# Attention, experts and a gated unit in one kernel: more weight blocks decoded beside the experts, splits and decoding put ahead of each chunk's results, six plain units for nine

## The chip, the cores and the metric

The kernel runs on one core of one Trainium2 chip. The metric is the device time of one execution in microseconds. Five engines work side by side, each through its own list of instructions in order: TensorE (PE: matmuls, with PEld for its weight loads), VectorE (DVE), ScalarE (ACT), GpSimd (POOL) and SyncE (SP), which here issues most of the DMA transfers. An engine that reaches an instruction whose data are not there waits, and so does everything behind it in its list.

## The reference

Causal attention with a decay bias over 4 x 8 heads of 576 positions, a layer that sends each of the 2304 rows to one of 8 experts, and a gated unit. Only the last two are touched:

```python
def _moe_ref(x, w_gate, w1, w2):            # x: 2304 x 512
    ...
    for e in range(E):                      # 8 experts
        xe = x[expert_idx == e]
        h = np.maximum(xe @ w1[e], 0.0)     # 512 x 1024
        ye = h @ w2[e]                      # 1024 x 512
        out[mask] = gate_w[mask, None] * ye

def _moe2_ref(x, w_gate, w_val, w_out, rms_g):
    xn = x / rms * rms_g
    g = xn @ w_gate                         # 512 x 1536
    silu = g * (1.0 / (1.0 + np.exp(-g)))
    val = xn @ w_val
    return (silu * val @ w_out).astype(np.float32)
```

`w_gate`, `w_val` and `w_out` of the gated unit arrive as 64-bit floats.

## The kernel before

**Stages.** Attention, then `moe` (expert 0, then `for s in range(1, E)`), then `glu` (the products with `w_gate` and `w_val` and the gating) and `glu_rest` (the product with `w_out`). On ACT, DVE and PE, and on SP for most of the program, the instructions stand in the order in which the Python code issues them. In `glu` each step is put into a plan with a due time by `add(at, ...)`, and the plan is issued in order of due time; POOL follows it there too.

**Every fp32 product is three passes** (`PASSES`): each operand is split into a rounded high part (a cast on ACT) and a rest (a subtraction on DVE or POOL, always called the rest here).

**Experts.** Expert s multiplies its `CAP[s-1]` rows (312, 304, 300, 292, 284, 268, 248) by w1 in eight `gemm1` groups f = 0..7 and by w2 in four `gemm2` chunks c = 0..3. In between the weights of expert s+1 come in eight pieces of 512 KB: `feed` issues a load into one of four staging buffers (`STG = 4`, used in turn), `split` casts a piece on ACT and calls `rest` for the piece before it on DVE. The rows of expert s+1 are transposed on PE after chunks 1 and 2 (`x_transpose`: high part on ACT, rest on DVE); `gemm1` of expert s+1 begins right after chunk 3 and needs all four column groups of them.

**64-bit blocks.** A block of 128 x 512 64-bit weights is loaded whole (512 KB) and made to 32-bit floats by `decoding`: four DVE operations (steps 0, 1, 3, 4) and an absolute value on ACT (step 2). Beside the experts `decode_words` takes blocks from the same staging buffers and sends the 32-bit result to DRAM (`keep_words`, 256 KB); five are done so before the change, one per expert 1 to 5. The remaining ones are decoded where they are used. The gated unit needs twelve pairs of blocks f = 0..11 (`w_gate` and `w_val`).

**Gated unit.** Rows are three groups p = 0..2 of 768. A unit (p, f) makes 128 columns of gate and value for one group. A plain unit does eight products of six matmuls (`WHOLE`); the other form does seven (`SEVEN`), with sums of x blocks (S1 to S4, `x_sums`, split by `x_rests`) and of weight blocks (`w_sum`), and adds up results on DVE (`glu_step`: u2, u3, c22, c21, c12). `PLAIN` lists the plain units; `UNITS` is the order. The list `START` gives the due times: 8 for a plain unit, 7 for the other. S1 lies in the buffer of A21, which plain units still read, and the sums of group 2 are made from a second load into the buffer of group 0 (`ringa`).

Of the kernel before, what the change touches and what calls it, by code (L numbers as in the profile page):

```python
# [7 lines left out]
F32 = mybir.dt.float32  # L8
# [11 lines left out]
E = 8  # L20
# [15 lines left out]
NF = F2 // 128  # L36
# [747 lines left out]
def keep_words(k, m, f, t):  # L784
    out = k.wo32[f // 2 - 2][:, f % 2, :] if m == 2 else k.wg32[:, m, :]
# [223 lines left out]
def moe(k, close):  # L1009
# [6 lines left out]
    k.order = [(s, u, q) for s in range(1, E) for u in range(4) for q in (0, 2)]  # L1016
# [53 lines left out]
    for s in range(1, E):  # L1070
# [50 lines left out]
WORDS_AT = 6 + 6  # L1121
# [6 lines left out]
A21 = S1  # L1128
PLAIN = ((0, 0), (0, 1), (1, 0), (1, 1), (2, 0), (2, 1), (0, 2), (1, 2), (2, 2))
UNITS = (list(PLAIN) + [(p, f) for f in range(3, NF - 2) for p in range(3)]  # L1130
# [124 lines left out]

def w_decode(k, f, n):
# [5 lines left out]
def w_parts(k, f):  # L1262
    if f == 0:
        return k.flat[:, 0, :], None, k.flat[:, 1, :], None
# [3 lines left out]
def w_sum(k, f, n):  # L1268
    g, gl, v, vl = w_parts(k, f)
# [90 lines left out]
def glu_head(k):  # L1360
    def dec(f, m, *parts):
        for n in parts:
            decoding(k, k.raw[f, m])[n]()

    V, G = k.nc.vector, k.nc.gpsimd
    k.raw, k.ps = {}, {}
    k.flat = staging(k, [2, 512], F32)
    k.nc.sync.dma_start(out=k.flat, in_=k.wg32)
    yield
    w_load(k, 1, 0)  # L1370
    yield
    w_load(k, 1, 1)
    yield
# [3 lines left out]
    yield  # L1377
    w_cast(k, 0, 0)
    yield
    dec(1, 0, 0, 1)  # L1380
    yield
    w_rest(k, 0, 0, G)
    dec(1, 0, 2)
    yield
    for n in (1, 4):
        w_cast(k, 0, n)
    yield
    dec(1, 0, 3, 4)
    for n in (1, 4):
        w_rest(k, 0, n, G)  # L1390
    yield
    yield
    yield
    x_cast(k, 0, "A11")
    x_rest(k, 0, "A11", V)
    dec(1, 1, 0, 1)
# [659 lines left out]
```

## Time and profile before

| | us |
|---|---|
| median of three timed runs | 848.31 (846.22 to 851.0) |
| profiled execution: its own time | 841.21 |
| its span | 839.5 |
| mean granted TensorE clock in it | 0.994 of full speed |

The span runs from the first to the last profiled instruction; 1.7 us of the execution lie around it. In the rows below, "idle before <-X" is the time an engine stood still before an instruction and what released it. PE's matmuls overlap at their ends, so the distance from one start to the next tells more than a duration.

### The profile page before, as it was taken

Reading aid. Unit: us, or ns where it says so; the run is one execution under the profiler, and the core shown is the slowest. Engines: PE = TensorE matmul, PEld = TensorE weight load, DVE = VectorE, ACT = ScalarE, POOL = GpSimd, SP = SyncE. Lnnn points to the kernel's source line nnn. Section 1 sums busy time; section 2 is a strip of 40 time slices with the busy share of each in tenths; the row PEclk is TensorE's granted clock in tenths of the full one; section 3 lists DMA queues with packets and bytes.
Section 4 is the critical chain, followed back from the end, with each engine's and each line's share of the span. In section 5 each row is a group of like instructions: output and inputs, shape, how many; then the busy total and the mean of one; then the engine's idle time right before and its main releaser. Section 6 shows DMA issues by size and latency. Waiting matters only on the chain.

```text
span 839.5 us, 15787 instructions
## 1 busy us (share of the span) xinstructions
PE 818.7 (98%) x5622; PEld 748.2 (89%) x5622; DVE 640.0 (76%) x1425; ACT 462.7 (55%) x1060; POOL 226.5 (27%) x249
## 2 busy tenths in 40 slices
PE   7999999999999999999999999999999999999994
PEld 4777767789899999999999999999999998899994
DVE  6557688965767767867698988888898969868880
ACT  5988988875756566566453443333333335453440
POOL 3335845342000000000131232544343352032120
PEclk9999999999999999999999999999999999999997
DMA  7999978246567576767651433323233375344510
GB/s 226 301 317 304 320 245 270 101 133 203 182 200 247 182 226 198 230 224 219 239 197 48 148 104 107 111 104 107 88 107 107 108 280 173 99 151 145 158 52 30
DMA packets 79757, 146.72 MB, mean 175 GB/s; under 512 B 7424, under 2 KB 44315, under 8 KB 79667
## 3 DMA queue, kind: packets, MB, share of 16 engines
q1 hardware_dynamic: 76707, 136.08, 51.1%
q0 software_dynamic: 2912, 9.46, 3.0%
q8 instruction: 46, 0.75, 0.4%
q14 instruction: 44, 0.36, 0.1%
q10 hardware_dynamic: 48, 0.07, 0.0%
HBM read 108.04 MB, written 37.54 MB: 173 GB/s over the span
## 4 chain that ended last, share of the span: by engine, by line
PE 92%; DVE 3%; ACT 1%; DMA 1%; issue 1%; SPq 0%; POOL 0%; POOLq 0%; ACTq 0%; DVEq 0%
PE gg L1314 29%; PE g L935 12%; PE g L912 12%; PE gp L1772 10%; PE go L1707 6%; PE t L370 5%; PE s L307 5%; PE pvy L416 5%; PE tl L444 2%; PE sm L338 2%; PE xp L883 1%; DMA ringa<-ytd 1%; PE r L984 1%; PE r L973 1%; ACT pt L403 0%
## 5 line engine op out<-in xcount | busy, mean ns | idle before, releaser
L935 PE MATMUL g<-h,u 128*128 128x256 f32 (+7 forms) x768 | 105.0, 295 | 0.0
L912 PE MATMUL g<-xt,u 128*128 128x256 f32 (+7 forms) x768 | 104.2, 295 | 0.0
L912 PEld LDWEIGHTS g<-xt,u 128*128 128x128 f32 x768 | 101.4, 189 | 0.8
L935 PEld LDWEIGHTS g<-h,u 128*128 128x128 f32 x768 | 101.2, 189 | 0.5
L1291 POOL TENSOR_TENSOR ws<-raw,ws 128x512 fp32r<-128x512 f32 (+1 forms) x25 | 33.0, 1335 | 220.4 <-ACT ws L1286 220.4
L744 ACT CAST u<-raw 128x1024 fp32r<-128x1024 f32 x62 | 65.1, 1050 | 19.5 <-DMA raw<-in_w 19.5
L351 ACT ACTIVATE p<-sc,nm 128x128 f32<-128x128 f32 (+3 forms) x128 | 71.3, 582 | 6.8 <-DVE nm L295 6.8
L757 DVE TENSOR_TENSOR u<-raw,u 128x1024 fp32r<-128x1024 f32 x58 | 70.5, 1218 | 0.4 <-ACT u L744 0.4
L1314 PE MATMUL gg<-gx2a,ws 128*128 128x384 f32 x360 | 67.4, 336 | 0.6 <-DVE tmp L1336 0.6
L1314 PE MATMUL gg<-gx0a,ws 128*128 128x384 f32 x360 | 67.7, 336 | 0.0
L1314 PE MATMUL gg<-gx1a,ws 128*128 128x384 f32 x360 | 67.1, 335 | 0.0
L1314 PEld LDWEIGHTS gg<-gx2a,ws 128*128 128x128 f32 x360 | 62.8, 188 | 0.9 <-DVE tmp L1336 0.9
L1314 PEld LDWEIGHTS gg<-gx0a,ws 128*128 128x128 f32 x360 | 63.1, 188 | 0.0
L1314 PEld LDWEIGHTS gg<-gx1a,ws 128*128 128x128 f32 x360 | 62.7, 188 | 0.0
L1352 POOL TENSOR_TENSOR hs<-tmp,hs 128x384 f32<-128x384 f32 x27 | 30.2, 1120 | 106.3 <-ACT hs L1350 106.3
L403 ACT COPY pt<-t 128x512 f32<-128x512 f32 (+3 forms) x160 | 56.1, 454 | 3.1 <-PE t L370 2.0
L370 PE MATMUL t<-ident,p 128*128 128x128 f32 x400 | 52.2, 275 | 0.0
L370 PEld LDWEIGHTS t<-ident,p 128*128 128x128 f32 x400 | 44.5, 140 | 8.4 <-DVE nm L295 8.3
L1693 POOL DMA_INDIRECT out<-raw,oid x18 | 20.5, 1139 | 111.9 <-DVE raw L1794 64.5
L416 PE MATMUL pvy<-pt,vp 128*64 128x512 f32 (+4 forms) x320 | 47.5, 428 | 0.7 <-ACT pt L403 0.7
L1332 ACT COPY tmp<-gg 128x384 f32<-128x384 f32 x27 | 13.0, 481 | 57.2 <-PE gg L1314 55.5
L1242 ACT ACTIVATE raw<-raw 128x512 f32<-128x512 f32 x31 | 21.2, 682 | 36.0 <-DVE raw L1240 35.9
(391 smaller groups left out, 1812.3 us busy)
## 6 DMA issues: line engine op xcount, KB each, us to landing
raw<-in_w SPq DMA_DIRECT2D x64, 512.0 KB
hd<-hs SPq DMA_DIRECT2D x72, 192.0 KB
xs<-zrow SPq DMA_DIRECT2D x8, 771.0 KB
raw<-in_wo SPq DMA_DIRECT2D x12, 512.0 KB
raw<-in_wg SPq DMA_DIRECT2D x12, 512.0 KB
raw<-in_wv SPq DMA_DIRECT2D x12, 512.0 KB
vp<-in_v SPq DMA_DIRECT2D x16, 320.0 KB
in<-cumd SPq DMA_DIRECT2D x20, 256.0 KB
```

The lines of the kernel that those rows point to most:

```text
L307: k.nc.tensor.matmul(ps[h], st.q[r, 128 * i:128 * i + 128], st.k[r, 0:w], start=True, stop=p >= BYPE)
L351: k.nc.scalar.activation(out, st.s[i, h][:, 0:w], AF.Exp, bias=st.nm[:, n:n + 1], scale=-1.0, accum_out=acc)
L370: nc.tensor.transpose(ps[:, off:off + 128], src[:, 128 * j:128 * j + 128], k.ident)
L403: nc.scalar.copy(b, a)
L416: nc.tensor.matmul(st.y[r, a - 64:512], st.v[:, h, j, :], k.pt[:, h, o:o + S - a], start=j == 0, stop=j == 4)
L744: nc.scalar.copy(w[:, :, 0, :], raw)
L757: k.nc.vector.tensor_tensor(w[:, :, 1, :], raw, w[:, :, 0, :].bitcast(F32), op=ALU.subtract)
L912: nc.tensor.matmul(ps[:, 0:n], w[:, f % 4, a, 128 * kc:128 * kc + 128], x[b][:, kc, 0:n], start=kc == 0 and i == 0, stop=kc == 3 and i == 2)
L935: nc.tensor.matmul(ps[:, 0:n], w[:, f % 4, a, 128 * c:128 * c + 128], k.h[b][:, f, 0:n], start=f == 0 and i == 0, stop=f == 7 and i == 2)
L1314: k.nc.tensor.matmul(k.ps[u, bank], w[:, a, 128 * c:128 * c + 128], x[:, b, GT * c:GT * c + GT], start=first and c == 0 and n == 0, stop=c ...
L1707: k.nc.tensor.matmul(k.acc[tau], c[:, a, 128 * t:128 * t + 128], w[:, b, :], start=f == 0 and i == 0, stop=f == NF - 1 and i == 2)
L1772: k.nc.tensor.matmul(k.acc[i, bank], t[:, a, j, :], item_weight(k, j, w, b), start=first and j == 0 and n == 0, stop=j == 5 and n == 2, sk ...
```

## The change

It has three parts.

**More blocks beside the experts.** Eleven blocks instead of five are decoded in `moe`: the three of `w_out` and both blocks of f = 0..3 (`WORDS = 4`). Experts 1 to 5 take two each, at c = 0 and c = 2, expert 6 takes one. The order of pieces (p) and blocks (w) is the string `PIECES_AND_WORDS`. In `glu`, f = 0..3 are then loaded as 32-bit floats (`words_load`).

**Order within an expert.** The split of a chunk, and steps 0 and 1 of a block, are now issued ahead of `gemm2` of the same chunk, so on ACT and DVE they stand ahead of that chunk's results; step 2 stands behind them, and steps 3 and 4 with the store at the next odd chunk.

**Six plain units.** (0, 2), (1, 2) and (2, 2) move from the plain form to the other one. The sums of x blocks, the weight sums of f = 2 and the second load for group 2 move some 20 due-time units ahead.

```diff
 def decode_words(k):
     s, m, f, raw = k.staged.pop(0)
-    for step in decoding(k, raw)[0:3]:
+    steps = decoding(k, raw)
+    for step in steps[0:2]:
         step()
+    yield
+    steps[2]()
     yield
     rest(k)
     compact(k, raw, raw)
...
-    words = [(E, 2, f) for f in range(4 + EARLY_OUT, NF)] + [(E, 0, 0), (E, 1, 0)]
-    for n, item in enumerate(words):
-        k.order.insert(WORDS_AT + 9 * n, item)
-    chain = iter(())
+    pieces = [(s, u, q) for s in range(1, E) for u in range(4) for q in (0, 2)]
+    words = [(E, 2, f) for f in range(4 + EARLY_OUT, NF)] + [(E, m, f) for f in range(WORDS) for m in range(2)]
+    k.order, chain = [(words if c == "w" else pieces).pop(0) for c in PIECES_AND_WORDS], iter(())
...
         for c in range(4):
+            if c % 2:
+                next(chain, None)
+            split(k, 1, c % 2 == 0)
+            if c % 2 == 0 and k.staged and k.staged[0][0] == E:
+                chain = decode_words(k)
+                next(chain)
             gemm2(k, s, c, n)
-            next(chain, None)
-            if c == 1:
-                split(k)
+            if c % 2 == 0:
+                next(chain, None)
...
-            split(k)
-            if c == 0 and s <= len(words):
-                chain = decode_words(k)
-                next(chain)
+            if c % 2:
+                feed(k)
+            if c == 1:
+                split(k)
...
-WORDS_AT = 6 + 6
+WORDS = 4
+PIECES_AND_WORDS = "pppppp" + "pp" + 5 * ("ppp" + "pwpppwp") + "ppp" + "pwpppp"
...
-PLAIN = ((0, 0), (0, 1), (1, 0), (1, 1), (2, 0), (2, 1), (0, 2), (1, 2), (2, 2))
+PLAIN = ((0, 0), (0, 1), (1, 0), (1, 1), (2, 0), (2, 1))
...
+def words_load(k, f):
+    k.val[f] = staging(k, [2, 512], F32)
+    k.nc.sync.dma_start(out=k.val[f], in_=k.wg32[f])
...
 def glu_head(k):
...
+    for f in range(3):
+        words_load(k, f)
+        yield
...
+    for f in range(2):
+        w_cast(k, f, 0)
+        yield
+        w_rest(k, f, 0, G)
...
+    x_sums(0, ("S3", "S1", "S2", "S4"), 1.0)
+    x_rests(0, (("S2", G),), 1.0)
+    x_rests(1, (("A11", V), ("A12", V), ("A21", V), ("A22", G)), 7.0)
+    x_rests(0, (("S3", V), ("S4", V)), 12.0)
+    x_rests(0, (("S1", V),), START[LAST[0]] + A21_AT)
...
+    x_sums(1, ("S3", "S1", "S2", "S4"), 18.0)
+    x_rests(1, (("S2", G), ("S3", V), ("S4", V)), 18.0)
     w_made(2)
...
+    w_split(2)
+    x_sums(2, ("S3", "S1", "S2", "S4"), done[0, "S1"] + 8.0)
+    x_rests(2, (("S2", V), ("S3", G), ("S4", V), ("S1", V)), START[LAST[2]] + A21_AT)
+    w_made(3)
+    w_split(3)
```

The order of DVE's instructions in chunks 1 to 3 of expert 5 (284 rows; the next one has 268). `sq` is a chunk's result, `xt` the rests of the next expert's transposed rows, `u` a rest of a weight piece, `raw_4641` the one block. Before:

```order
L1243 TENSOR_SCALAR raw_4641<-raw_4641 128x512
L1244 SCALAR_TENSOR_TENSOR raw_4641<-raw_4641 128x512
L887 TENSOR_TENSOR xt_4790<-xp_0_4791,xt_4789 128x268
L887 TENSOR_TENSOR xt_4790<-xp_1_4792,xt_4789 128x268
L757 TENSOR_TENSOR u_4785<-raw_4683,u_4785 128x2x512
L943 TENSOR_TENSOR sq_4716<-sq_4716 128x284
L887 TENSOR_TENSOR xt_4790<-xp_2_4844,xt_4789 128x268
L887 TENSOR_TENSOR xt_4790<-xp_3_4845,xt_4789 128x268
```

And now, with `raw_4673` the first and `raw_4839` the second block:

```order
L1251 TENSOR_SCALAR raw_4673<-raw_4673 128x512
L1252 SCALAR_TENSOR_TENSOR raw_4673<-raw_4673 128x512
L946 TENSOR_TENSOR sq_4754<-sq_4754 128x284
L890 TENSOR_TENSOR xt_4820<-xp_0_4821,xt_4819 128x268
L890 TENSOR_TENSOR xt_4820<-xp_1_4822,xt_4819 128x268
L757 TENSOR_TENSOR u_4789<-raw_4715,u_4789 128x2x512
L757 TENSOR_TENSOR u_4789<-raw_4749,u_4789 128x2x512
L1247 TENSOR_SCALAR raw_4839<-raw_4839 128x512
L1248 SCALAR_TENSOR_TENSOR raw_4839<-raw_4839 128x512
L946 TENSOR_TENSOR sq_4754<-sq_4754 128x284
L890 TENSOR_TENSOR xt_4820<-xp_2_4884,xt_4819 128x268
L890 TENSOR_TENSOR xt_4820<-xp_3_4885,xt_4819 128x268
```

The first two operations of the second block now stand ahead of the last two rests `xt`, so these wait for that block's load.

SP's transfers over the same chunks; `wg_65` is the 32-bit copy in DRAM, `in_w` an expert's weights, `in_wg` a 64-bit block. Before:

```order
L786 DMA wg_65<-raw_4641 128x512
L729 ISA
L729 DMA raw_4783<-in_w 128x1024
L729 ISA
L729 DMA raw_4787<-in_w 128x1024
```

And now:

```order
L786 DMA wg_65<-raw_4673 128x512
L729 ISA
L729 DMA raw_4787<-in_w 128x1024
L1234 DMA raw_4839<-in_wg 128x1024
L729 ISA
L729 DMA raw_4843<-in_w 128x1024
```

The store of the first block is followed by the load of a piece, and that by the load of the second block. With four buffers in turn the second block gets the buffer of the first (`raw_4673`, `raw_4715`, `raw_4749`, `raw_4787`, then `raw_4839`), so its load goes out when the store has read that buffer.

DVE at the first unit of seven products, before (unit (0, 3)); `ringa` rows are sums of group 2, `gg` a unit's results:

```order
L1354 TENSOR_TENSOR hs_5512<-gg_6181,hs_5512 128x384
L1206 TENSOR_TENSOR ringa_5223<-ringa_5223 128x768 x3
L1334 TENSOR_TENSOR tmp_6159<-gg_6208,tmp_6159 128x384
L1346 TENSOR_TENSOR hs_5513<-gg_6198,hs_5513 128x384
L1336 TENSOR_TENSOR tmp_6159<-gg_6208,tmp_6159 128x384
```

And now (unit (0, 2)):

```order
L1370 TENSOR_TENSOR hs_5560<-gg_5990,hs_5560 128x384
L1225 TENSOR_TENSOR gx2b_5797<-ringa_5271,gx2b_5797 128x768
L1225 TENSOR_TENSOR gx2a_5563<-ringa_5271,gx2a_5563 128x768
L1350 TENSOR_TENSOR tmp_5893<-gg_6019,tmp_5893 128x384
L1362 TENSOR_TENSOR hs_5559<-gg_6009,hs_5559 128x384
L1352 TENSOR_TENSOR tmp_5893<-gg_6019,tmp_5893 128x384
```

The sums of group 2 no longer stand between the last plain unit's results and the new unit's first one; two rests of that group do.

## Rows read from the trace of the kernel before

**Rows 1.** The page, head and part 1: busy us (share) xinstructions.

```profile
span 839.5 us, 15787 instructions
...
PE 818.7 (98%) x5622; PEld 748.2 (89%) x5622; DVE 640.0 (76%) x1425; ACT 462.7 (55%) x1060; POOL 226.5 (27%) x249
```

**Rows 2.** Windows: experts 1 to 7, six plain units, units of seven products.

```profile
core 0: us, PE busy (x) PEld busy (x) DVE busy (x) ACT busy (x) POOL busy (x), PEclk, DMA share, GB/s
225.30:416.20 190.90, 190.90 (x1430) 186.74 (x1429) 138.79 (x213) 116.61 (x227) 2.72 (x3) 1.00 0.68 217
416.20:466.56 50.36, 50.36 (x292) 50.32 (x291) 43.54 (x66) 23.05 (x40) 11.68 (x9) 1.00 0.44 147
...
491.53:691.20 199.67, 198.55 (x1137) 196.64 (x1136) 169.13 (x307) 71.18 (x138) 85.45 (x73) 1.00 0.34 117
```

**Rows 3.** Timeline of PE in the gated unit: start, us, what.

```profile
449.93 16.80 PE L1314 MATMUL gg<-gx2a,ws 128*128 128x384 f32 x96
466.56 8.49 PE L1314 MATMUL gg<-gx0a,ws 128*128 128x384 f32 x48
...
496.13 1.31 PE L1314 MATMUL gg<-gx0b,ws 128*128 128x384 f32 x6 [0.26 <-DVE tmp L1334]
...
538.25 2.25 PE L1314 MATMUL gg<-gx0a,ws 128*128 128x384 f32 x12
...
560.11 2.25 PE L1314 MATMUL gg<-gx0a,ws 128*128 128x384 f32 x12
```

**Rows 4.** Groups by line, experts 1 to 7: decoding, xcount | busy us, mean ns.

```profile
L1240 DVE SCALAR_TENSOR_TENSOR raw<-raw 128x512 uint32<-128x512 uint32 x7 | 4.9, 695 | 0.2
L1244 DVE SCALAR_TENSOR_TENSOR raw<-raw 128x512 uint32<-128x512 uint32 x7 | 4.9, 694 | 0.2
...
L1242 ACT ACTIVATE raw<-raw 128x512 f32<-128x512 f32 x7 | 4.7, 674 | 3.0 <-DVE raw L1240 3.0
...
L1243 DVE TENSOR_SCALAR raw<-raw 128x512 f32<-128x512 f32 x7 | 3.4, 482 | 0.0
...
L1239 DVE TENSOR_SCALAR raw<-raw 128x512 uint32<-128x512 uint32 x7 | 3.0, 425 | 3.7 <-DMA raw<-in_wv 1.6 <-DMA raw<-in_wo 1.3 <-DVE u L757 0.9
```

**Rows 5.** Timeline of PE, expert 5: chunks 0 and 1, then the next expert's gemm1.

```profile
353.58 6.48 PE L935 MATMUL g<-h,u 128*128 128x284 f32 x48
...
368.33 3.11 PE L912 MATMUL g<-xt,u 128*128 128x268 f32 x24
```

**Rows 6.** Timeline of SP, expert 5: the store of the decoded block.

```profile
363.51 0.33 SPq L786 DMA_DIRECT2D wg<-raw  x1
```

**Rows 7.** Timeline of ACT, expert 5: chunk 0's copy, casts of x, a piece.

```profile
356.92 0.40 ACT L937 COPY y<-g 128x284 f32<-128x284 f32 x1 [2.51 <-PE g L935]
...
365.11 0.67 ACT L886 CAST xt<-xp 128x268 fp32r<-128x268 f32 x2
...
371.69 1.05 ACT L744 CAST u<-raw 128x1024 fp32r<-128x1024 f32 x1 [1.25 <-DMA raw<-in_w]
```

**Rows 8.** Timeline of DVE, expert 5: the block's first step, two rests.

```profile
357.65 0.43 DVE L1239 TENSOR_SCALAR raw<-raw 128x512 uint32<-128x512 uint32 x1 [1.55 <-DMA raw<-in_wv]
...
365.63 0.77 DVE L887 TENSOR_TENSOR xt<-xp,xt 128x268 fp32r<-128x268 f32 x2
```

**Rows 9.** Timelines of expert 3: ACT, SP, PE and ACT, as in rows 5 to 7.

```profile
300.09 0.41 ACT L937 COPY y<-g 128x300 f32<-128x300 f32 x1 [2.83 <-PE g L935]
...
306.88 0.33 SPq L786 DMA_DIRECT2D wo<-raw  x1
...
312.05 3.42 PE L912 MATMUL g<-xt,u 128*128 128x292 f32 x24
...
314.19 1.06 ACT L744 CAST u<-raw 128x1024 fp32r<-128x1024 f32 x1 [0.96 <-DMA raw<-in_w]
```

**Rows 10.** Timeline of DVE, gated unit: sums of x blocks, two rests.

```profile
454.76 1.94 DVE L1206 TENSOR_TENSOR ringa<-ringa 128x768 f32<-128x768 f32 x2
...
471.41 3.47 DVE L1217 TENSOR_TENSOR gx1b<-tmp,gx1b 128x768 fp32r<-128x768 f32 x2
```

More of the change, by code (lines that the diff above doesn't have):

```diff
@@ L1014, in rank @@
             next(k.last, None)
-    k.order = [(s, u, q) for s in range(1, E) for u in range(4) for q in (0, 2)]
-    words = [(E, 2, f) for f in range(4 + EARLY_OUT, NF)] + [(E, 0, 0), (E, 1, 0)]
-    for n, item in enumerate(words):
-        k.order.insert(WORDS_AT + 9 * n, item)
-    chain = iter(())
+    pieces = [(s, u, q) for s in range(1, E) for u in range(4) for q in (0, 2)]
+    words = [(E, 2, f) for f in range(4 + EARLY_OUT, NF)] + [(E, m, f) for f in range(WORDS) for m in range(2)]
+    k.order, chain = [(words if c == "w" else pieces).pop(0) for c in PIECES_AND_WORDS], iter(())
+    assert not pieces and not words
     row = ids(k, k.x[0], EARLY)
@@ L1128 @@
 A21 = S1
-PLAIN = ((0, 0), (0, 1), (1, 0), (1, 1), (2, 0), (2, 1), (0, 2), (1, 2), (2, 2))
-UNITS = (list(PLAIN) + [(p, f) for f in range(3, NF - 2) for p in range(3)]
+PLAIN = ((0, 0), (0, 1), (1, 0), (1, 1), (2, 0), (2, 1))
+UNITS = (list(PLAIN) + [(p, f) for f in range(2, NF - 2) for p in range(3)]
          + [(0, NF - 2), (1, NF - 2), (0, NF - 1), (1, NF - 1), (2, NF - 2), (2, NF - 1)])
@@ L1360, in glu_head @@
 def glu_head(k):
-    def dec(f, m, *parts):
-        for n in parts:
-            decoding(k, k.raw[f, m])[n]()
     V, G = k.nc.vector, k.nc.gpsimd
[L1366 to L1373, printed above, removed]
+    k.raw, k.ps, k.val, k.scr = {}, {}, {}, {}
+    for f in range(3):
+        words_load(k, f)
+        yield
     for g in range(2):
@@ L1376, in glu_head @@
     yield
[L1377 to L1396, printed above, removed]
-    yield
-    x_cast(k, 0, "A12")
-    dec(1, 1, 2)
-    x_rest(k, 0, "A12", V)
-    dec(1, 1, 3, 4)
-    yield
-    x_cast(k, 0, "A21")
-    x_rest(k, 0, "A21", V)
-    yield
-    x_cast(k, 0, "A22")
-    x_rest(k, 0, "A22", G)
-    yield
+    for f in range(2):
+        w_cast(k, f, 0)
+        yield
+        w_rest(k, f, 0, G)
+        yield
+        for n in (1, 4):
+            w_cast(k, f, n)
+        yield
+        for n in (1, 4):
+            w_rest(k, f, n, G)
+        yield
+    for b in ("A11", "A12", "A21", "A22"):
+        x_cast(k, 0, b)
+        x_rest(k, 0, b, V)
+        if b == "A21":
+            w_sum(k, 2, 0)
+        elif b == "A22":
+            w_sum(k, 2, 1)
+        yield
 def glu(k):
@@ L1467, in glu @@
         add(8.0 + 0.1 * g, glu_load, k, g)
-    x_rests(1, (("A11", V), ("A12", V), ("A21", V), ("A22", G)), 8.1)
     load, over, sent = {2: 0.5, 3: 6.5}, {}, {}
     def w_made(f):
-        whole = (0, f) in PLAIN
-        for m in range(2):
-            add(load[f] + 0.1 * m, w_load, k, f, m)
-        for n in range(8):
-            t = fill(load[f] + 6.0)
-            add(t, w_decode, k, f, n)
-        for n in range(0 if whole else 4):
+        t = load[f] + 4.0
+        if f >= WORDS:
+            for m in range(2):
+                add(load[f] + 0.1 * m, w_load, k, f, m)
+            for n in range(8):
+                t = fill(load[f] + 6.0)
+                add(t, w_decode, k, f, n)
+        elif f > 2:
+            add(load[f], words_load, k, f)
+        for n in range(2 * (f == 2), 4):
             t = fill(t)
@@ L1483, in w_split @@
     def w_split(f):
-        whole = (0, f) in PLAIN
         end = last[f - 2] + 1
@@ L1487, in w_split @@
         t = v = at
-        for n, eng in ((0, V), (4, G), (1, V)) if whole else ((0, V), (2, G), (3, G), (1, V)):
+        for n, eng in ((0, V), (2, G), (3, G), (1, V)):
             if eng is V:
```

42 lines of the change are left out of this document (16 added, 26 removed).

## The prediction

> **What bounds the kernel now.** I read the page's busy times first, then windows by stage, then the timeline of each engine at the places that the change touches. TensorE is busy 818.7 us of a span of 839.5 [rows 1]. By stage it is closer still: beside experts 1 to 7 it is busy for 190.90 of 190.90 us, over the first six plain units for 50.36 of 50.36, and over the units of seven products for 198.55 of 199.67, all at full granted clock [rows 2]. So in the stages that change, time is won only by taking matmuls away, and lost as soon as TensorE must wait for something. VectorE is the engine to watch: it is busy 43.54 of the 50.36 us of the plain units and 138.79 of 190.90 beside the experts [rows 2].
>
> The sum below is made against the profiled execution, 841.21 us with its span of 839.5. The three timed runs lie 5 to 10 us above it, with a median of 848.31; I carry the difference over to that median.
>
> **First part: three units with seven products instead of eight.** From one pair of plain units to the next TensorE's timeline goes from 449.93 to 466.56, which is 8.315 us a unit, 48 matmuls of 173 ns [rows 3]. With seven products, three units in a row take from 538.25 to 560.11, or 7.287 us each [rows 3]. Three units times 1.03 us is 3.1 us less. The same from the other side: 18 matmuls fewer at 173 ns are 3.1 us. TensorE has no idle time beside them that could swallow this, so the 3.1 us count in full. Since the plain form uses TensorE longest, this is also all that the form of the units can give.
>
> **What those units ask of VectorE earlier.** All sums and splits of x for groups 0 and 1 must now be ready six units into the stage and not nine. Over the six plain units VectorE loses the decoding of four blocks (both of f = 2 and of f = 3). A block costs it 0.425 + 0.695 + 0.482 + 0.694 = 2.3 us [rows 4], so 9.2 us go. It gains four sums of group 2 (1.94 us for two, 3.9 in all), less one sum of group 0 that moves ahead of the stage (0.97) [rows 10]. It also gains the two rests of group 1 that now stand earlier (3.47 together [rows 10]), the rest of S1 of group 0 and two of group 2, and one weight sum. I bound each of these four by half a sum and by half of the 3.47, 0.5 to 1.7, so 2 to 7 us. The balance lies between 0.8 us less and 4.2 more; I take 1.5 more, near the sums. That leaves VectorE busy some 45 of 50.4 us, and the cost is nothing: what hides it is TensorE's own 50 us of plain products. The bound at the upper end is 47.7 of 50.4, still inside. Without that cover each us beyond would be a us of TensorE.
>
> One place is tight. Before the first unit of seven products VectorE now does two rests of group 2. The unit's second product must be read (u2) before its fifth product writes the same bank, four products or 4.2 us after the unit begins. VectorE needs the last plain result, the two rests and u2 itself: about 0.2 + 0.55 + 2 x (0.95 to 1.74) + 0.55, or 3.2 to 4.8 us, the middle term from [rows 10]. So TensorE waits 0 to 0.6 us there. Today it waits 0.26 us at the same step [rows 3]; there three sums of group 2 stand ahead of it on VectorE, and these are made one to two units earlier now. I set new and old against each other: 0, between 0.3 less and 0.4 more.
>
> **Second part: six more blocks decoded beside the experts.** That is 6 x 2.3 = 13.8 us of VectorE, which goes from 138.8 to 152.6 busy of 190.9, and 6 x 0.67 us of ScalarE [rows 2, 4]. As load this is hidden. What may not be hidden is a chain. In experts 1 to 5 the second block's first two operations stand on VectorE ahead of the rests of the last two column groups of the next expert's rows, and its absolute value stands on ScalarE ahead of their casts. The next `gemm1` needs these groups. Behind the block wait, on each of the two engines, chunk 2's evictions and these groups. And the block's load can only go out when the first block's store has read the shared buffer; on SP two pieces' loads stand behind it, for casts a chunk later and beyond, which have that time to spare.
>
> The chain for expert 5, the shortest of the five. Chunk 0's copy begins at 356.92 [rows 7]. The first block's load ends VectorE's wait at 357.65 [rows 8]. Steps 0 and 1 take 1.12 us, the absolute value 0.67, steps 3 and 4 take 1.18 [rows 4]: with the handing over the store goes out at 360.7, where today it goes out at 363.51 [rows 6]. Today too the second load behind that store takes its buffer, and the cast that waited for this load began at 371.69 [rows 7]: 8.18 us from store to landing. In expert 3 the same pair of rows gives 314.19 - 306.88 = 7.31 us [rows 9]. So the second block is there between 368.0 and 368.9. Then come two steps (1.12), the absolute value (0.67), the cast (0.67 for two groups) and the rest (0.77 for two) [rows 4, 7, 8]; the third group is through 2.8 us after the landing, at 370.8 to 371.7. `gemm1` began at 368.33 and needs that group after six matmuls of 0.13 us, at 369.1 [rows 5]. TensorE would wait 1.7 to 2.6 us.
>
> The same for expert 3: copy 300.09, store at 302.7 (its first block is there in time), landing 310.0 to 310.9, third group at 312.8 to 313.7; needed at 312.05 + 6 x 0.143 = 312.9 [rows 9]. TensorE would wait 0 to 0.8 us. Experts 1 and 2 have longer chunks and lie below that, expert 4 between 3 and 5. If expert 5's first block came as early as expert 3's, its store would go out at 359.6 and the wait would be 0.5 us. The sum over the five lies between 0.5 us and about 5 us. I take 1.7, expert 5 alone with the shorter transfer: the 8.18 us was the longest of the five.
>
> Here a page of the Trainium skill speaks for less. The row is 7.31 to 8.18 us from a 256 KB store to the landing of a 512 KB load behind it [rows 6, 7, 9]. "DMA: Bandwidth & Descriptors", section "Anatomy of one DMA — SWDGE (gpsimd) path", gives about 2.0 us fixed plus the bytes over 436 GB/s for one transfer (on another issuing path than here); an estimate from it is 2.6 + 3.2 = 5.8 us, and then expert 5's wait would be about 0.2 us and the sum 2.9 us less than today instead of 1.4. No load in these rows is that quick, since a piece is in flight between the two.
>
> **Third part: pieces cast ahead of a chunk's results.** ScalarE waits for pieces today while it has chunk results behind it (1.25 and 0.96 us in the two rows [rows 7, 9]). Cast one chunk earlier, a piece is waited for while TensorE still works on the chunk; a result held up by a us or two then costs a bank for that time, and TensorE goes on into others. I price it at nothing; without that cover it would cost a part of those two waits per expert, up to 2 us.
>
> **Sum.** 3.1 less, 0 at the turn, 1.7 more: 1.4 us less, 839.8 for the profiled execution and 846.9 us on the scale of the median. That is 0.17%; the three runs lie 0.56% apart, and a change under 0.5% (4.2 us) can hardly be told from none.
>
> **Rivals.**
> (a) The second block comes early enough everywhere: in expert 5 it would have to land by 369.1 - 2.8 = 366.3, 5.6 us after the store. The experts stay without a wait, and the 3.1 us remain, less up to 0.5: 845.5 us. For it speaks that the store goes out nearly 3 us earlier than today, when fewer loads are in flight; against it the measured 7.31 and 8.18. The page of the Trainium skill named above comes close to this case.
> (b) The second block is late in every expert and the kernel gets slower. Each us by which the landing slips beyond the table above costs about 5 us, one per expert. From 7.3 us of waits on, 1.5 a expert, it is slower by more than 0.5%; at 2 us late each, 10 us, the time is 855. For it speaks that about a tenth more bytes pass beside the experts (6 x 0.75 MB on 217 GB/s x 190.9 us = 41 MB), where the transfers already fill 0.68 of the DMA engines' time [rows 2]; against it, that four of the five have slack.
> (c) VectorE isn't ready at the turn: sums or splits for the first units of seven products lag and TensorE stands for about what was saved. 848 to 850 us. For it speaks a VectorE that is busy 86% there, against it the balance of the moved work.
> (d) TensorE has reserves in the experts that its busy time hides, and the earlier splits set them free. 843 us or less. Against it speaks that not one wait of TensorE is recorded there.
>
> **Chances.** The forecast 0.45, (a) 0.20, (b) 0.13, (c) 0.14, (d) 0.08. The forecast's own range is 845 to 849. Over all cases I give 842.5 to 851.5 us, which takes in the 0.5 and 5 us of waits and the scatter of the runs. Faster by over 0.5% come out of (d), a part of (a) and a little scatter, 0.18; slower out of (b) and a little of (c) and scatter, 0.17; within 0.5% is left with 0.65.
>
> **What would show it.** In the new profile the distance between units must be 8.3 us six times and then 7.3, with 18 matmuls fewer. Between experts TensorE must show a wait for `xt` of 1 to 3 us at the start of expert 6, little at the others, and the second block's first step must begin about 7 us after the store. If there are no such waits, the step on the transfer was wrong; if they stand at every expert, its size was. If TensorE stands over 0.6 us around the first unit of seven products, the balance of VectorE was wrong.

## The result, and the profile after

The changed kernel takes 854.91 us (median of six runs, 853.65 to 858.96), the kernel before in the same set 848.28. The ratio is 1.0083, with a 95% interval of 1.0059 to 1.0107: 0.8% slower, where 846.9 us and no measurable change were forecast. The profiled execution took 858.96 us, that of before 841.21; they lie 4.1 us above and 7.1 us below their medians, so stages are compared here, and not the two spans. The stage ahead of expert 1, which the change does not touch, alone takes 227.42 us in the one and 222.45 in the other; in the profiles further below it is 221.5 to 223.7 us in the sets of runs where the kernel before takes 842 us, and 227 to 231 where it takes 848 to 850.

First the page, head and part 1 (to set beside [rows 1]), and the windows over experts 1 to 7 and over the six plain units of the changed kernel, with the columns of [rows 2].

```profile
span 857.2 us, 15800 instructions
...
PE 824.9 (96%) x5604; PEld 748.0 (87%) x5604; DVE 648.8 (76%) x1439; ACT 465.2 (54%) x1064; POOL 238.4 (28%) x255
```

```profile
227.42:436.68 209.26, 200.29 (x1447) 191.43 (x1445) 148.59 (x234) 124.13 (x238) 6.30 (x6) 0.99 0.70 223
436.68:487.04 50.36, 50.36 (x292) 50.32 (x291) 46.18 (x63) 24.06 (x40) 14.32 (x7) 1.00 0.42 136
```

The window over the experts in [rows 2] begins 2.85 us into expert 1. From its first product on, the kernel before has:

```profile
222.45:416.20 193.75, 193.39 (x1446) 188.97 (x1445) 140.42 (x216) 118.94 (x231) 2.72 (x3) 1.00 0.68 216
```

There are 18 matmuls fewer, as the change says, and yet TensorE is busy longer. The plain units take 50.36 us as before. The loss lies beside the experts: from the first product of expert 1 to the first of the gated unit it is 209.26 us, where before has 193.75. Of these 15.5 us more, TensorE is recorded busy for 6.9, with as many matmuls, and idle for the rest. Behind the experts, from the first plain unit to the end of the span, it is 857.2 - 436.68 = 420.5 us, where before has 839.5 - 416.20 = 423.3, so 2.8 us are won there.

TensorE's timeline in the gated unit (to set beside [rows 3]) shows the second and third pair of plain units, the first unit of seven products, and three units further on.

```profile
453.77 16.80 PE L1330 MATMUL gg<-gx1a,ws 128*128 128x384 f32 x96
470.40 16.80 PE L1330 MATMUL gg<-gx2a,ws 128*128 128x384 f32 x96
487.04 1.21 PE L1330 MATMUL gg<-gx0a,ws 128*128 128x384 f32 x6
...
511.56 2.25 PE L1330 MATMUL gg<-gx0a,ws 128*128 128x384 f32 x12
...
533.42 2.25 PE L1330 MATMUL gg<-gx0a,ws 128*128 128x384 f32 x12
```

A pair takes 16.63 us, that is 8.3 a unit, and three units of seven products take 21.86, as before. So the saving is there, 2.8 of the 3.1 us in this profile. A part of what eats it can be seen where expert 5 begins. The timeline of TensorE there, and the chain of work that led up to it, in order of time (start, us, what):

```profile
351.23 0.95 PE L915 MATMUL g<-xt,u 128*128 128x284 f32 x6
354.46 4.42 PE L915 MATMUL g<-xt,u 128*128 128x284 f32 x18 [2.27 <-ACT xt L889]
```

```profile
343.35 2.39 DMA wg<-raw
...
345.75 6.40 DMA raw<-in_wg
...
352.27 0.44 DVE raw L1247
...
352.74 0.70 DVE raw L1248
...
353.46 0.67 ACT raw L1250
354.13 0.28 ACT xt L889
...
354.44 0.47 DVE xt L890
```

Read it from the end: six products are done, then `gemm1` waits for the third column group of x. Its cast and rest stand behind the second block's first three operations, and these behind the block's load, which went out when the first block's store had left the buffer. The store's issue, 343.35, is 3.75 us behind chunk 0's copy (339.60); the load lands 8.80 us behind the store. In this profile such waits for `xt` cost 5.6 us in three places, at the start of experts 3, 5 and 6. The stage is 15.5 us longer, though, so they are not the whole loss. A second profile of the same kernel has 203.02 us beside the experts, 9.3 more than before, and only one such wait, of 1.17 us. One kernel so gives lengths 6 us apart from one execution to the next.

### The profile page after: what moved, and what is told of

The parts are those of the page before. It is cut to its first block, busy times and chain, and to the rows that moved or that the text cites. A ratio compares the mean times of both kernels' runs of the same rounds, so it can differ in the third digit from the quotient of the medians.

```text
span 857.2 us, 15800 instructions
## 1 busy us (share of the span) xinstructions
PE 824.9 (96%) x5604; PEld 748.0 (87%) x5604; DVE 648.8 (76%) x1439; ACT 465.2 (54%) x1064; POOL 238.4 (28%) x255
## 4 chain that ended last, share of the span: by engine, by line
PE 75%; DVE 10%; DMA 9%; ACT 4%; issue 1%; SPq 0%; POOL 0%; POOLq 0%; DVEq 0%; ACTq 0%
PE gg L1330 30%; PE gp L1767 10%; PE go L1702 6%; PE t L370 5%; PE s L307 5%; PE pvy L416 5%; PE g L915 5%; DVE u L757 3%; PE g L938 3%; DMA raw<-in_wg 3%; DMA raw<-in_wv 2%; PE tl L444 2%; PE sm L338 2%; DMA raw<-in_w 1%; DMA wg<-raw 1%
## 5 line engine op out<-in xcount | busy, mean ns | idle before, releaser
L915 PE MATMUL g<-xt,u 128*128 128x256 f32 (+7 forms) x768 | 108.2, 299 | 6.2 <-ACT xt L889 5.6
L1307 POOL TENSOR_TENSOR ws<-raw,ws 128x512 fp32r<-128x512 f32 (+1 forms) x26 | 36.5, 1422 | 229.3 <-ACT ws L1302 227.0
L1368 POOL TENSOR_TENSOR hs<-tmp,hs 128x384 f32<-128x384 f32 x30 | 33.9, 1130 | 121.4 <-ACT hs L1366 121.4
L1330 PE MATMUL gg<-gx2a,ws 128*128 128x384 f32 x336 | 63.8, 336 | 0.6 <-DVE tmp L1352 0.6
L1330 PE MATMUL gg<-gx0a,ws 128*128 128x384 f32 x336 | 63.9, 336 | 0.0
L1330 PE MATMUL gg<-gx1a,ws 128*128 128x384 f32 x336 | 63.2, 335 | 0.0
L1330 PEld LDWEIGHTS gg<-gx2a,ws 128*128 128x128 f32 x336 | 58.6, 188 | 0.9 <-DVE tmp L1352 0.9
L1330 PEld LDWEIGHTS gg<-gx0a,ws 128*128 128x128 f32 x336 | 59.0, 188 | 0.0
L1330 PEld LDWEIGHTS gg<-gx1a,ws 128*128 128x128 f32 x336 | 58.6, 188 | 0.0
L919 DVE SCALAR_TENSOR_TENSOR h<-g,h 128x256 fp32r<-128x256 f32 (+7 forms) x64 | 26.5, 447 | 25.7 <-ACT h L918 25.6
```

Source lines behind the costliest of these rows:

```text
L915: nc.tensor.matmul(ps[:, 0:n], w[:, f % 4, a, 128 * kc:128 * kc + 128], x[b][:, kc, 0:n], start=kc == 0 and i == 0, stop=kc == 3 and i == 2)
L1330: k.nc.tensor.matmul(k.ps[u, bank], w[:, a, 128 * c:128 * c + 128], x[:, b, GT * c:GT * c + GT], start=first and c == 0 and n == 0, stop=c ...
```

## The experiments

A block is called first or second by its place in the expert. Each ratio is against the kernel before in the same set of runs. The lengths of the experts are the distances between the first products of one expert and of the next, from one profile of each kernel. They hold for that one execution: the profiled execution of x_ahead took 849.56 us where its median is 845.00, so its 204.18 is some 4.6 us too long to go with its ratio. Kernels one_block, loads_only, second_bare and half_pieces leave out a part of the work, as their texts say.

The expected texts count in microseconds on the scale of 848.3 for the kernel before. It took 841.8 us in the set of order_alone, one_block, second_bare and second_late and in that of loads_only, x_ahead and the two runs with stores by GpSimd, and 847.6 to 849.9 in the others, so compare by ratios. Theories have letters in these texts. T: the second block lands late, and what the next `gemm1` needs is queued behind it on VectorE and ScalarE. V and D: the additional transfers cost, wherever they stand. O: the new order costs. G: the gated unit loses its gain at the turn to seven products. Q: stores that wait on SyncE hold back the loads behind them. R: one load more in a ring of four buffers leaves each too little lead.

| kernel | ratio [95%] | experts 1 to 7 | 3 | 4 | 5 | 6 | 7 |
|---|---|---|---|---|---|---|---|
| before | 1 | 193.75 | 29.25 | 28.48 | 27.80 | 25.40 | 22.47 |
| order_alone | 0.9998 [0.9988, 1.0008] | 193.75 | 29.25 | 28.48 | 27.81 | 25.39 | 22.47 |
| one_block | 0.996 [0.9945, 0.9975] | 194.12 | 29.25 | 28.48 | 27.81 | 25.39 | 22.84 |
| loads_only | 0.9984 [0.9975, 0.9993] | 195.36 | 29.25 | 28.48 | 27.97 | 26.47 | 22.83 |
| second_bare | 1.003 [1.0018, 1.0042] | 199.94 | 30.09 | 28.76 | 29.19 | 26.11 | 25.42 |
| second_late | 1.005 [1.0035, 1.0065] | 199.95 | 29.48 | 28.81 | 28.67 | 28.49 | 24.16 |
| after, second time | 1.0096 [1.0064, 1.0127] | 203.02 | 29.48 | 29.32 | 29.90 | 29.23 | 24.75 |
| half_pieces | 1.0072 [1.0052, 1.0091] | 205.42 | 30.14 | 29.54 | 32.19 | 29.00 | 23.48 |
| second_ahead | 1.0052 [1.0036, 1.0067] | 201.24 | 29.98 | 29.51 | 29.96 | 27.98 | 23.43 |
| x_ahead | 1.0039 [1.0026, 1.0051] | 204.18 | 30.58 | 30.36 | 28.95 | 27.56 | 24.07 |
| store_pool | 1.0233 [1.0219, 1.0246] | 216.17 | 31.80 | 32.30 | 31.83 | 29.25 | 28.57 |
| x_ahead_late | 1.002 [1.0005, 1.0035] | 197.21 | 29.24 | 28.92 | 29.06 | 26.37 | 23.27 |
| ten_late | 1.0006 [0.9988, 1.0024] | 196.88 | 29.25 | 28.48 | 28.86 | 27.11 | 22.83 |
| nine_mixed | 0.9979 [0.9964, 0.9995] | 195.04 | 29.25 | 28.48 | 28.47 | 25.40 | 22.89 |

### The parts one by one

**The order alone**: the kernel before with the new order of splits and decoding, and nothing else. The loop over the chunks is that of the diff ahead of the prediction; the list of pieces and blocks becomes

```diff
-WORDS_AT = 6 + 6
+PIECES_AND_WORDS = "pppppp" + "pp" + 5 * ("ppp" + "pwpppp") + "ppp" + "ppppp"
```

> The kernel before with only the new order in the experts: pieces cast and the block's first two operations ahead of a chunk's products, one block per expert, nine plain units. Theory T: nothing, 847.5 to 849 us. Rival O: 850 to 854 us, with TensorE waiting in the experts. The mechanism of reserves (earlier splits set TensorE free) would give 845 us or less.

0.9998, and the experts have the same length to 0.01 us. The order costs and brings nothing while there is one block per expert; the mechanism of reserves, rival (d), falls.

**One block**, with the changed gated unit:

```diff
-    words = ... + [(E, m, f) for f in range(WORDS) for m in range(2)]
+    words = ... + [(E, 0, 0), (E, 1, 0)]
-PIECES_AND_WORDS = "pppppp" + "pp" + 5 * ("ppp" + "pwpppwp") + "ppp" + "pwpppp"
+PIECES_AND_WORDS = "pppppp" + "pp" + 5 * ("ppp" + "pwpppp") + "ppp" + "ppppp"
-    k.nc.sync.dma_start(out=k.val[f], in_=k.wg32[f])
+    k.nc.sync.dma_start(out=k.val[f], in_=k.wg32[0])
```

> The changed kernel with one block per expert as before; the gated unit reads the words of f = 0 for f = 1 to 3 too (output wrong there), so its own work and loads are those of the changed kernel. Theory T: the six plain units bring their 3.1 us and the order of the splits costs nothing, 845 to 846 us. Rival O (splits ahead of the chunk's results cost ScalarE's waits): 847 to 850 us. Rival G (the gated unit loses its 3.1 us again at the turn): about 848 us, with waits of TensorE around the seventh unit.

0.996: 0.4% of the set's 841.84 us are 3.4 us. The six plain units bring what was worked out, 3.1, within the interval, and the turn costs nothing that can be told from none.

**The second block without decoding**, its load and its store left in:

```diff
+    if (m, f) in SECOND:
+        yield
+        yield
+        rest(k)
+        keep_words(k, m, f, raw)
+        feed(k)
+        yield
+        return
```

> The changed kernel, with the second block of experts 1 to 5 replaced by 512 KB of an expert's weights, loaded in the same place and stored in the same place without the five operations of decoding (the output is then wrong in the gated unit). All transfers stay, and the operations and what waits in front of them go. Theory T: no wait for xt, 845 to 848 us. Rival D (the additional transfers are what costs): 852 to 856 us.

1.003, which is 850.8 on the scale of the forecast and between the two theories. No operation of a second block is left, and yet 2.5 us are lost against before and 5.9 against one_block. Theory T alone falls here.

**The second block's operations later**: its start moved behind the transposes.

```diff
-            if c % 2 == 0 and k.staged and k.staged[0][0] == E:
+            second = c == 2 and s < E - 1
+            if c % 2 == 0 and not second and k.staged and k.staged[0][0] == E:
...
             gemm2(k, s, c, n)
...
                 if c in (1, 2):
                     x_transpose(k, s + 1, (2 * c - 2, 2 * c - 1), tiles_of(CAP[s]))
...
+            if second and k.staged and k.staged[0][0] == E:
+                chain = decode_words(k)
+                next(chain)
+                next(chain)
```

> The changed kernel, with the second block's first three operations moved behind the transposes, casts and rests of the next expert's rows in chunk 2; block, load, store and glu stay. Theory T (the second block lands late, and what the next gemm1 needs is queued behind it on VectorE and ScalarE): the waits for xt of up to 2.3 us at the first products of each expert go, and of the 9.7 us that the second blocks cost (854.9 against 848.3 less 3.1) at least 6 come back: 845 to 849 us. Rival V (the additional transfers or VectorE's additional operations slow the experts wherever they stand): 853 to 856 us, with waits elsewhere.

1.005, between T's 0.996 to 1.001 and V's 1.006 to 1.009. TensorE's waits beside the experts are now these and two of 0.4 us and less (who waited for whom: total, times, longest; `ms` is the product that sums up the squares `sq` of a chunk's result):

```profile
PE ms L960 <- DVE sq L946: 2.6, 3, 1.8
...
PE g L915 <- DVE xt L890: 0.2, 1, 0.2
```

The waits for ScalarE's `xt` are gone as T said, but about half of the loss stays. The longest wait for `ms` was 0.5 and 0.8 us in the two profiles of the changed kernel and is 1.8 here; chunk 3's squares now stand behind the operations that moved.

### Bytes, chain or queue

**Half pieces**: three of eight pieces at half the size.

```diff
-            k.nc.sync.dma_start(out=raw, in_=src[:, q:q + 2, :])
+            m = 1 if s > 1 and q == 2 and u else 2
+            k.nc.sync.dma_start(out=raw[:, 0:m, :], in_=src[:, q:q + m, :])
+            if m == 1:
+                raw = raw[:, 0:1, :].broadcast_to((128, 2, 512))
```

> The changed kernel, in which three of the eight pieces of weights of experts 2 to 7 are loaded by half (256 KB less each; cast and rest read the half twice, so they cost the same and the output is wrong). 768 KB less per expert is what the second block's load and store add; order, operations and the chain of the second block are those of the changed kernel. Theory V (the transfers beside the experts, pieces and blocks together, come late because there are more bytes): nearly all of the loss in the experts goes, 0.995 to 0.999 of the kernel before, and the waits for xt and ms with it. Theory T (the chain of store, load and decoding is late by its own length): most of it stays, 1.004 to 1.010.

> The changed kernel once more, as the comparison of this set: 1.006 to 1.011 of the kernel before, with waits for xt at the first products of experts 3, 5 and 6 and for ms beside them.

1.0072 against 1.0096, with intervals that overlap, and the transfers run at 204 GB/s beside the experts instead of 223. The experts are no shorter, 205.42 us against 203.02. Theory V asked for 0.995 to 0.999, so the amount of data is not the main thing that makes the loads late; a gain of a few us the intervals leave open.

**The second block's load ahead of the first store**, into the buffer of an earlier piece:

```diff
     rest(k)
+    ahead = bool(k.order) and k.order[0][0] == E
+    if ahead:
+        feed(k)
     compact(k, raw, raw)
     keep_words(k, m, f, raw)
-    feed(k)
+    if not ahead:
+        feed(k)
...
-... 5 * ("ppp" + "pwpppwp") ...
+... 5 * ("ppp" + "pwppwpp") ...
```

> The changed kernel, with the second block's load ahead of the first block's store and into another buffer, one place sooner, and the piece that stood there cast behind the transposes of chunk 2. Theory T: the load no longer waits for the store, the second block lands 3 us or more earlier, the waits for xt go and the time is 0.997 to 1.002 of before. Theory V: the piece that changed places with it is late instead, waits move to ms and to later pieces, and it stays at 1.003 to 1.008.

1.0052. It mends about as much as moving the operations, and no more. That is the time, and with 3.0 us of waits for `ms` and none for ScalarE's `xt` also the sign, that the rival V of this text gave: the piece that changed places is late instead. So it counts in which order SyncE issues. Its timeline (SPq marks transfers), first of the changed kernel from the first block's store of expert 4 on, then of one_block at the start of the same expert 5:

```profile
343.35 0.33 SPq L786 DMA_DIRECT2D wg<-raw  x1
343.95 0.33 SPq L729 DMA_DIRECT2D raw<-in_w  x1
345.75 0.34 SPq L1234 DMA_DIRECT2D raw<-in_wg  x1
346.38 1.37 SPq L729 DMA_DIRECT2D raw<-in_w  x2
357.48 0.33 SPq L786 DMA_DIRECT2D wg<-raw  x1
358.07 0.33 SPq L729 DMA_DIRECT2D raw<-in_w  x1
359.19 0.31 SPq L865 DMA_DIRECT2D tokd<-ids  x1
359.71 0.36 SPq L729 DMA_DIRECT2D raw<-in_w  x1
360.26 0.93 SPq L823 DMA_DIRECT2D x<-xs  x2
```

```profile
339.74 0.35 SPq L729 DMA_DIRECT2D raw<-in_w  x1
340.31 0.94 SPq L823 DMA_DIRECT2D x<-xs  x2
```

From 347.8 to 357.48 nothing is issued: the second block's store is next in the queue and waits, first for the block's load, which landed at 352.15, then for VectorE's decoding. Behind it stand two pieces and the rows of the next expert. These go out 9.0 us after expert 5 began (351.23), in one_block 0.7 us after (339.58). The two largest waits of SyncE at stores beside the experts, of the changed kernel, and then the largest of one_block:

```profile
SPq L786 <- DVE raw L1252: 37.7, 10, 5.4
SPq L786 <- DMA raw<-in_wg: 14.0, 4, 4.5
```

```profile
SPq L786 <- DVE raw L1252: 16.2, 5, 3.4
```

With the smaller ones the stores wait 59.1 us, eleven of them, against 17.4 us for five. The sum by itself is no measure of the loss, though. SyncE's waits for the buffers of pieces went down at the same time, from 74.6 us in one_block to 45.3, and nine_mixed below, which loses 1.3 us beside the experts, still has 33.2 us of waits for decoding in nine stores. What counts is which loads stand behind a waiting store, and how soon they are needed. That is theory Q, and four runs tried it.

**Loads only**: one_block, and in the second block's place a load of 512 KB that nobody decodes or stores.

```diff
-... 5 * ("ppp" + "pwpppp") ...
+... 5 * ("ppp" + "pwpppnp") ...
...
+    if m < 0:
+        yield
+        yield
+        rest(k)
+        feed(k)
+        yield
+        return
```

> One block per expert and the glu of the run with one block (0.996 of before; its words are those of f = 0), and in the second block's place in experts 1 to 5 a load of 512 KB of weights that is neither decoded nor stored, in the same ring of four buffers. Theory Q: no second store on SyncE, hence nearly the time of the run with one block, 0.996 to 0.998. Theory R (a ring of four buffers with one more load in it gives each load too little lead, whoever decodes or stores): 1.000 to 1.003, where the run with the second load and store without decoding stood.

0.9984, just above what Q allows and below R, and 2 us above one_block. The additional load costs that; the other 3.9 of the 5.9 us between one_block and second_bare come with the stores (and the block in expert 6, which second_bare has too).

**The next rows ahead of the second store**:

```diff
-        else:
+        elif s == 1:
             load_x(k, s + 1)
...
+                if c == 2 and s + 2 < E:
+                    load_x(k, s + 2)
```

> The changed kernel, with the loads of the next expert's rows issued at the end of chunk 2, ahead of the second block's store on SyncE instead of behind it. Theory Q: ScalarE's 9 us of waits for x go, the second block's place stays; 1.003 to 1.008 of the kernel before (1.009 as changed). If the rows are not what is late: 1.008 to 1.011.

1.0039, where the changed kernel stands at 1.008 to 1.010: the move of two loads gives back about half of what was lost against before. This rests on the ratios; the one profile, an execution well above the median, has no shorter experts. ScalarE's waits for these rows beside the experts were 0.8 us in the kernel before and in the changed kernel the first line below; in x_ahead there is none. SyncE's timeline at the same place shows the rows 6.7 us ahead of the store:

```profile
ACT x L870 <- DMA x<-xs: 9.0, 6, 2.0
```

```profile
344.36 1.01 SPq L823 DMA_DIRECT2D x<-xs  x2
351.09 0.36 SPq L786 DMA_DIRECT2D wg<-raw  x1
```

**Stores issued by GpSimd**, so that SyncE never waits for a decoded block:

```diff
-    k.nc.sync.dma_start(out=out, in_=...)
+    q = k.nc.sync if m == 2 and f < 4 + EARLY_OUT else k.nc.gpsimd
+    q.dma_start(out=out, in_=...)
```

> The changed kernel, with the blocks' stores beside the experts issued by GpSimd, which has nothing else to do there, instead of by SyncE. Theory Q (SyncE issues in order, each store waits there for VectorE's decoding, 37.7 us in ten waits against 16.2 in five with one block, and all loads behind it, pieces and the next rows, go out late): the loads that share no buffer with a block go out earlier, 0.998 to 1.005 of the kernel before. Theory T (the second block's own load waits for the first store by its buffer, wherever that is issued): the waits for xt stay and so does most of the loss, 1.005 to 1.010.

1.0233, outside both expectations. The chain of work ahead of expert 5 shows a part of it:

```profile
340.99 4.39 DMA wg<-raw
...
345.44 3.71 DMA raw<-in_wg
```

The store keeps the buffer for 4.39 us and not 2.39, and SyncE now waits in order for the buffers, 49.5 us in eleven waits for `wg<-raw` and `wo<-raw`, with the same loads behind it, where the changed kernel has 8.5 in seven. So SyncE's queue is held up all the same, and this run does not test Q by itself; that the longer hold is the whole of the loss is not shown. With the late operations it is better, but still worse than with SyncE's stores, and again outside both expectations:

> Stores issued by GpSimd and, besides, the second block's first operations behind the transposes of chunk 2. Theory Q and T together: SyncE no longer holds loads back and VectorE and ScalarE no longer stand in front of xt; 0.996 to 1.000 of the kernel before, the experts within 3 us of the kernel before. If loads still wait by their buffers: 1.002 to 1.005, as with the late second block alone (1.005).

1.0103 [1.0081, 1.0124], experts 205.93 us.

### Towards a version that wins

**Both moves**: next rows ahead of the store, operations behind the transposes.

> Both moves together on the changed kernel: the next rows loaded ahead of the second block's store, and the second block's first operations behind the transposes of chunk 2. Alone they gave 1.004 and 1.005 of the kernel before, against 1.009. If they mend different losses (SyncE's queue there, VectorE's queue here): 0.997 to 1.001. If both mend the same lateness: 1.003 to 1.005.

1.002, between the two expectations, and the experts up to 3 have the length of before. **Next rows and second block's load both ahead**:

> The next rows loaded ahead of the second store, and the second block loaded ahead of the first store into another buffer (alone 1.005). If the two mend different losses: 0.998 to 1.002, otherwise 1.003 to 1.005.

1.0025 [1.0014, 1.0037], experts 197.55 us. Alone the moves gave 1.0039, 1.005 and 1.0052, so they overlap in part and mend different losses in part.

**Nine blocks, late**: second blocks in experts 1 to 3 only.

```diff
-WORDS = 4
+WORDS = 3
-... 5 * ("ppp" + "pwpppwp") + "ppp" + "pwpppp"
+... 3 * ("ppp" + "pwpppwp") + 3 * ("ppp" + "pwpppp")
```

> Nine blocks instead of eleven beside the experts: second blocks in experts 1 to 3 alone (there the chunks are longest), moved behind the transposes as in the run with the late second block; f = 3 is decoded in the gated unit. Theory V: the short experts 4 and 5 are free of second blocks and lose nothing, so the experts cost 0 to 3 us and the 3 us of the six plain units remain: 0.996 to 1.000 of before. If the loss comes with each second block alike, three fifths of the 6 to 7 us stay, 1.001. If the decoding of f = 3 is late in the gated unit, TensorE waits at its first products there, 1.002 or more.

1.0009 [0.9996, 1.0023], experts 198.13 us, of which 3.5 us too many in expert 7 alone (26.01 us). In its gated unit the last splits of f = 3 stand behind the first products with them, which so use old words; its time says nothing of that stage.

**Both moves and ten blocks**: none in expert 6, the value words of f = 3 decoded in the gated unit.

```diff
-... 5 * ("ppp" + "pwpppwp") + "ppp" + "pwpppp"
+... 5 * ("ppp" + "pwpppwp") + "ppp" + "ppppp"
             add(load[f], words_load, k, f)
+            add(load[f] + 0.1, w_load, k, f, 1)
+            for n in (2, 3, 6, 7):
+                t = fill(load[f] + 6.0)
+                add(t, w_decode, k, f, n)
```

> As the run with both moves, but ten blocks instead of eleven: the one in expert 6 goes, and the value words of f = 3 are decoded in the gated unit. If a block in the shortest chunks (experts 6 and 7 were 6 us longer in the changed kernel's second profile) costs by its place: 2 to 4 us less than with both moves alone, 0.993 to 0.998 of the kernel before, and the first products of f = 3 without a wait. If that loss only comes down from experts 3 to 5: the same time as with both moves.

1.0006. Against both moves alone the block in expert 6 is worth 0.3 us beside the experts and 0.1% in time, within the intervals, so the loss there seems to come down from expert 5. In the last run that expert's second block goes too, and the value words of f = 1 are decoded at the head of the gated unit:

```diff
-PIECES_AND_WORDS = ... 5 * ("ppp" + "pwpppwp") + "ppp" + "ppppp"
+PIECES_AND_WORDS = ... 4 * ("ppp" + "pwpppwp") + "ppp" + "pwpppp" + "ppp" + "ppppp"
```

> Both moves, and nine blocks: second blocks in experts 1 to 4 alone, none in expert 6; the value words of f = 1 are decoded beside experts 6 and 7 at the head of the gated unit, those of f = 3 in it. In the run with ten blocks experts 1 to 4 had the length of the kernel before and expert 5 was 1.1 us, expert 6 1.7 us and expert 7 0.4 us longer. If these come from the second block of expert 5, they go, 0.996 to 0.999 of the kernel before. If the experts 6 and 7 lose as much by the block that is decoded there, 1.000 to 1.002.

0.9979 [0.9964, 0.9995]: 1.8 us less than the kernel before, with an interval that only just leaves out no change. Expert 6, for which neither run has a block in its list, has its 25.40 us again and not 27.11, so its loss did come down from expert 5. Of the kernels here that do the whole computation it is the only one faster than the kernel before. TensorE's waits beside its experts are down to two:

```profile
PE ms L960 <- DVE sq L946: 0.4, 1, 0.4
PE yt L1004 <- ACT hr L997: 0.4, 1, 0.4
```

## Why the prediction was wrong

**The first part was right.** 3.1 us less were worked out; 0.9998 to 0.996 (order_alone to one_block) are 3.2 us, and the units take the 8.3 and 7.3 us of before. **The turn and VectorE's balance were right**: 45 of 50.4 us were forecast for the plain units, 46.18 is measured. Around the first unit of seven products no wait of TensorE is recorded, and further on 0.6 us is the longest. Rival (c) falls.

**The third part, at nothing, was right for one block per expert** (order_alone). With two it seems to have a price, since the loads come later: in the second profile ScalarE stood at a cast in expert 5 with chunk 2's results behind it. What that costs no run takes apart.

```profile
376.17 1.05 ACT L744 CAST u<-raw 128x1024 fp32r<-128x1024 f32 x1 [3.97 <-DMA raw<-in_w]
377.12 0.39 ACT L940 COPY y<-g 128x284 f32<-128x284 f32 x1
```

**The second part failed**, at one step: "on SP two pieces' loads stand behind it, for casts a chunk later and beyond, which have that time to spare". The links of the chain that I did count are nearly right. In expert 5, for which they were worked out, the changed kernel has these rows of ScalarE, SyncE, VectorE and TensorE:

```profile
371.98 0.40 ACT L940 COPY y<-g 128x284 f32<-128x284 f32 x1 [0.27 <-PE g L938]
...
375.75 0.33 SPq L786 DMA_DIRECT2D wg<-raw  x1
...
383.50 0.43 DVE L1247 TENSOR_SCALAR raw<-raw 128x512 uint32<-128x512 uint32 x1 [3.36 <-DMA raw<-in_wg]
...
385.67 2.85 PE L915 MATMUL g<-xt,u 128*128 128x268 f32 x18 [1.40 <-ACT xt L889]
```

The store comes 3.77 us after chunk 0's copy (forecast 3.8), the second block's first step 7.75 us after the store (7.31 to 8.18), and TensorE waits 1.40 us (1.7). That is the wait that was to show at the start of expert 6. But the transfer is longer in some of the other experts. From the store to the first step it is 6.9, 9.1, 6.9, 8.9 and 7.8 us in experts 1 to 5, and TensorE also waits 1.95 and 2.27 us behind the two long ones, experts 2 and 4, where less than in expert 5 was forecast. The sum of 5.6 us lies a little above the bound of about 5, that of the second profile, 1.2, below the 1.7. Since 9.3 and 15.5 us were lost beside the experts, these waits are the smaller part.

What is missing is the queue. The second store waits on SyncE for a block that itself came behind the first store, and two pieces and the next expert's rows wait with it. I looked at the first two loads behind the second block's and took their time to spare as given. The store and the loads behind it were not counted: the rows went out 9.0 us into expert 5, with one block 0.7 us. Nor did I count that an expert hands its delay on to the next, whose chunks are shorter: without the second block in expert 5, expert 6 is 1.7 us shorter (ten_late to nine_mixed).

The ladder of runs gives the sizes on the scale of 842 us: the six plain units -3.4 (one_block), the additional load +2.0 (loads_only), the second store on SyncE with expert 6's block +3.9 (second_bare), the second block's operations where they stand +4 to +6 (after). So against the 1.7 of the forecast stand +4 to +6, and beside them two terms, +2.0 and +3.9, that were put at nothing. The last two are not independent: x_ahead takes about 0.5% off without touching a store or an operation, second_late 0.4%, both together 0.7%.

Rival (b) named the time, 855, but not the cause, and that it met the median was in part luck. It had 2 us late in every expert; in the second profile experts 1 and 2 keep their 30.8 and 29.6 us, and even expert 7 is 2.3 us longer. It argued with the additional bytes, and half_pieces shows that 768 KB less per expert give back a few us at most. The Trainium skill, "DMA: Bandwidth & Descriptors", section "Anatomy of one DMA — SWDGE (gpsimd) path", gave an estimate of 2.6 us for the store and 3.2 for the load, for transfers issued by GpSimd. For SyncE's this trace has 2.39 and 6.40, so the store comes close and the load, with others in flight, takes twice as long; GpSimd's own store in store_pool took 4.39.

How much of the remaining 2 us of loads_only comes from the ring and how much from the load itself stays open; a fifth buffer was not tried. Open too is how much of the 3.9 is the block in expert 6.

## What to carry to other kernels

When a step is added whose store waits for a computation, list every transfer behind it on the issuing queue up to the next expert, not the next two, and ask when each is needed; moving the loads that depend on nothing ahead of it was worth as much as moving the computation itself. A stage whose work units shrink can take the added step in its long units and not in its short ones, so cost it unit by unit. The recorded waits of the bottleneck engine can be far smaller than the loss (4.6 of 9.3 us in the second profile), therefore measure the length of the stage first, in more than one profile.

## What was not expected of the hardware

A 256 KB store issued by GpSimd held its buffer for 4.39 us, the same store by SyncE for 2.39 us (2.1 to 2.7 in the five experts). After the wait in expert 5 the granted clock of TensorE fell to 0.62 between 354.46 and 359.00, and 18 matmuls took 4.42 us; in half_pieces, after a wait of 2.21 us at the same place, it stayed at 1.00. The windows of the two, changed kernel first:

```profile
354.46:359.00 4.54, 4.45 (x21) 4.18 (x21) 3.69 (x7) 2.31 (x6) 0.00 (x0) 0.62 0.16 60
```

```profile
351.08:354.49 3.41, 2.88 (x18) 2.44 (x18) 3.38 (x7) 2.51 (x6) 0.00 (x0) 1.00 0.02 5
```

That is a stretch partly at the lower of the clock's two levels (0.50 is granted from 355.0 to 358.0), and it cost about 1.5 us once (2.97 us for the same 18 matmuls in half_pieces). In the changed kernel's own profile the clock stayed at 1.00 after the waits of 1.95 and 1.40 us. What decides it no run here shows.
